# Attention, then two gated layers: scores of two of four sequences from fp16 pairs, thresholds of three sequences moved to VectorE

## The chip, the core and the metric

One NeuronCore of a Trainium2 chip runs the whole program. TensorE (PE) multiplies matrices into PSUM; VectorE (DVE), ScalarE (ACT) and GpSimd (POOL) do the elementwise work; SyncE (SP) issues the DMAs. Each engine takes its own instructions in the order in which they stand, and waits on semaphores for the others. The metric is the device time of one execution in microseconds; lower is better.

## The reference, cut to what matters

```python
scores = q @ k.T / sqrt(64)                  # 4 sequences, 8 heads, 576 positions, 64 wide
keep   = scores >= rowmax(scores) - tau      # tau = 0.02
attn   = where(keep, exp(scores - rowmax), 0); attn /= sum(attn)
x      = (attn @ v) laid out as 2304 tokens x 512
h = x @ w_in;  g = h * clip(h + 3, 0, 6) / 6;  x = g @ w_out      # 512 -> 2048 -> 512
h = x @ w_in2; g = max(h, 0) ** 2;             out = g @ w_out2
```

A score that falls on the wrong side of the threshold changes an output row, so the scores need close to fp32 accuracy. One pass of 16-bit products isn't enough for that: wherever 16-bit numbers are multiplied, each operand is split into a high and a low part.

## The kernel before, in words

**Attention.** A unit is one pair of heads of one sequence, 16 units in all, four to a sequence (`u.b` is the sequence, counted from 0). A unit has nine jobs: four tiles of 128 query rows for each head, and one job for the last 64 rows of both heads. A job is `scores` (PE, tile `s`), `soft1` (DVE takes the row minimum `nm` of the negated scores, the threshold `thr` is `nm` plus tau, ACT takes the exponential `e`), `soft2` (DVE masks and sums; ACT and POOL split the result into two fp16 parts `p`, a DMA transposes them into `pt`), and five jobs later `av` (PE, tile `o`).

For sequence one the scores are plain fp32 products (L291). For sequences two to four `prep_steps` (L187) transposes k and q on PE (`tps`) and splits each from PSUM into a high part (ACT) and a low part (DVE) of type fp32r; high times high, low times high and high times low are then two matmuls for each half of the columns, so four in a job and eight in the job of the last rows (L295): 40 in a unit. Two DMAs copy the high part of k onto the other 64 partitions. `prep_v` (L238) finds the largest |v| of the unit with a reduce, an fp32 matmul (`vm`) and a second reduce, and makes a power of two of it, `vsc`.

**The layers.** They run block by block (layer 1 and layer 2 of sequence one, then of sequence two, ...), each in groups: `hidden` (PE, tile `hp`, 24 matmuls of 288 columns, fp16 pairs) and `output` (PE, tile `y`, 24 matmuls). At the end of layer 1, the boundary below, VectorE has to take the largest |y| of each of the four tiles of `ya` (L730) and of all (L733), PE spreads it over the partitions (L119), DVE makes a power of two of it (L121, L126, L737), and only then ACT and DVE split `ya` into `x` (L386, L387), without which the first `hp` of layer 2 can't begin.

**The order.** The loops issue some attention jobs between the steps of the layers (`attn_to`). A scheduler that works from a simulated timeline then orders each engine's instructions, so an instruction without waiting inputs can stand far ahead of its place in the source. Up to 378 us the weights are decoded as well (L544 to L623): 32 blocks through ACT, DVE and POOL. Scores, `hp` and `y` share three PSUM buffers, `tps`, `vm`, `o` and the rest two others.

Of the kernel before, what the change touches and what calls it, by code (L numbers as in the profile page):

```python
# [39 lines left out]
def attention_moe_moe_kernel(  # L40
# [195 lines left out]
    vscs = {}  # L236

    def prep_v(u):  # L238

# [11 lines left out]
        nc.vector.tensor_scalar(out=sc, in0=sc, scalar1=2.0 ** -100, scalar2=2.0 ** -13, op0=ALU.max, op1=ALU.mult)
        nc.vector.reciprocal(out=sc, in_=sc)
        nc.vector.tensor_scalar(out=sc.bitcast(I32), in0=sc.bitcast(I32), scalar1=0x7f800000, scalar2=None, op0=ALU.bitwise_and)
# [603 lines left out]
```

## Time and profile before

| | us |
|---|---|
| median of 3 runs | 1099.24 (1097.81 to 1100.69) |
| the profiled execution | 1097.44 |
| its span, first to last instruction | 1095.7 |
| PE busy | 1014.6 (93%) |
| ACT, DVE, POOL busy | 654.4, 642.9, 502.0 |

The page divides the span into 40 slices; a digit is the busy share in tenths. "Granted clock" is the share of full speed that TensorE was given. A line of a timeline says when an instruction started, how long it took and, in brackets, how long its engine had been idle and what ended that. Times of consecutive matmuls overlap in the records, so what a matmul costs is read from one start to the next.

### The profile page before, as it was taken

The numbers are of one execution on the slowest core, as the hardware profiler recorded it, in microseconds if no ns is written. First come the engines' busy times: TensorE is split into PE (matmuls) and PEld (weight loads), VectorE is DVE, ScalarE is ACT, GpSimd is POOL, SyncE is SP. The second block draws the span as 40 slices with busy tenths as digits, with TensorE's granted clock in tenths as the row PEclk, the third lists the DMA queues.
The fourth block names the chain that finished last, engine by engine and source line by source line (L and its number), as shares of the span: only waits on it lengthen the run. The fifth ranks groups of instructions, "written<-read, shape, count | busy, mean of one in ns | idle before, by whom it ended". The sixth has DMA issues, their size and how long they took to land.

```text
span 1095.7 us, 23283 instructions
## 1 busy us (share of the span) xinstructions
PE 1014.6 (93%) x9248; PEld 819.2 (75%) x9248; DVE 642.9 (59%) x1344; ACT 654.4 (60%) x1128; POOL 502.0 (46%) x629
## 2 busy tenths in 40 slices
PE   6877698897987999999999999999999999998998
PEld 4655476676776888888788888888788887776776
DVE  6885789889778875455855554555834231233122
ACT  5896798877887875655675555655654243313222
POOL 5886656755656754344355334443444222212111
PEclk9999799898988999999999999999999999999999
DMA  9999689896877686656565555555464342222211
GB/s 271 186 181 234 197 313 289 253 215 175 198 190 213 144 200 168 146 119 150 127 139 125 141 143 140 132 130 133 94 139 116 105 121 83 92 77 78 78 39 44
DMA packets 258748, 167.58 MB, mean 153 GB/s; under 512 B 215888, under 2 KB 228176, under 8 KB 258640
## 3 DMA queue, kind: packets, MB, share of 16 engines
q1 hardware_dynamic: 257072, 165.71, 60.3%
q8 instruction: 72, 1.18, 0.4%
q10 hardware_dynamic: 1568, 0.39, 0.2%
q14 instruction: 36, 0.29, 0.1%
HBM read 98.57 MB, written 21.50 MB: 110 GB/s over the span
## 4 chain that ended last, share of the span: by engine, by line
PE 72%; DVE 13%; DMA 7%; ACT 5%; issue 2%; POOL 1%; ACTq 0%; POOLq 0%; DVEq 0%
PE hp L685 30%; PE y L722 30%; PE s L295 4%; PE o L350 4%; DMA pt<-p 2%; DVE nm L301 2%; DVE wc L620 2%; DMA wd<-in_moe_w_out_dram 1%; DVE e L318 1%; DMA vraw<-in_v_dram 1%; PE s L291 1%; DVE ya L728 1%; PE tps L180 1%; DMA pt<-wpo 1%; DMA wd<-in_moe_w_in_dram 1%
## 5 line engine op out<-in xcount | busy, mean ns | idle before, releaser
L685 PE MATMUL hp<-x,wpi 128*128 128x288 f16 x3072 | 405.7, 291 | 13.8 <-ACT wpi L622 5.2
L685 PEld LDWEIGHTS <-wpi 128*128 128x128 f16 x3072 | 300.1, 99 | 94.7 <-ACT wpi L622 5.5
L722 PEld LDWEIGHTS <-wpo 128*128 128x128 f16 x3072 | 297.5, 99 | 92.7 <-DVE e L318 7.9
L722 PE MATMUL y<-gh,wpo 128*128 128x288 f16 x2048 | 338.7, 288 | 15.9 <-DVE e L318 7.5
L696 POOL TENSOR_TENSOR gl<-g,gh 128x576 f16<-128x576 f32 x128 | 168.6, 1318 | 299.6 <-ACT gh L695 298.9
L722 PE MATMUL y<-gl,wpo 128*128 128x288 f16 x1024 | 209.2, 288 | 0.0
L301 DVE TENSOR_REDUCE nm<-s 128x1 f32<-128x576 f32 x144 | 107.6, 750 | 58.7 <-PE s L295 55.3
L728 DVE SCALAR_TENSOR_TENSOR ya<-y,yq,ya 128x576 f32<-128x576 f32 (+1 forms) x97 | 77.9, 809 | 97.5 <-PE y L722 97.3
L326 POOL TENSOR_TENSOR p<-e,p 128x512 f16<-128x512 f32 x108 | 127.2, 1178 | 0.0
L695 ACT ACTIVATE gh<-g 128x576 f16<-128x576 f32 x128 | 86.9, 680 | 56.0 <-DVE g L693 27.9
L318 DVE SCALAR_TENSOR_TENSOR e<-s,thr,e 128x576 f32<-128x576 f32 x108 | 87.9, 814 | 38.9 <-ACT e L311 38.0
L324 ACT ACTIVATE p<-e 128x576 f16<-128x576 f32 x108 | 73.5, 681 | 51.3 <-DVE e L318 41.1
L350 PE MATMUL o<-v,pt 128*128 128x64 f16 (+1 forms) x2016 | 90.5, 200 | 12.2 <-ACT os L357 4.0
L350 PEld LDWEIGHTS <-pt 128*128 128x128 f16 x2016 | 80.6, 101 | 24.1 <-issue 9.3
L295 PE MATMUL s<-k_st,q_st 128*128 128x288 f32 x480 | 94.5, 320 | 0.6 <-DVE g L690 0.3
L693 DVE TENSOR_TENSOR g<-g,hp 128x576 f32<-128x576 f32 x64 | 48.0, 750 | 64.6 <-ACT g L692 64.4
L690 DVE SCALAR_TENSOR_TENSOR g<-g,r_w,hp 128x576 f32<-128x576 f32 x64 | 51.9, 810 | 57.8 <-ACT g L689 57.7
L689 ACT ACTIVATE g<-hp,r_h,aq 128x576 f32<-128x576 f32 x64 | 52.9, 829 | 53.7 <-PE hp L685 52.9
L692 ACT ACTIVATE g<-hp,r_w 128x576 f32<-128x576 f32 x64 | 47.1, 736 | 57.1 <-PE hp L685 55.9
L311 ACT ACTIVATE e<-s,nm 128x576 f32<-128x576 f32 x108 | 78.5, 727 | 0.4
L325 POOL TENSOR_TENSOR p<-e,p 128x64 f16<-128x64 f32 x108 | 35.2, 326 | 95.0 <-issue 59.2
L333 POOL TENSOR_SCALAR sm<-sm,vsc 128x2 f32<-128x2 f32 (+1 forms) x80 | 23.0, 287 | 112.7 <-DVE e L318 99.7
(127 smaller groups left out, 1138.5 us busy)
## 6 DMA issues: line engine op xcount, KB each, us to landing
wpi<-scr SPq DMA_DIRECT2D x48, 512.0 KB, 3.7
wpo<-scr SPq DMA_DIRECT2D x48, 512.0 KB, 4.1
wd<-in_moe_w_in_dram SPq DMA_DIRECT2D x16, 1024.0 KB, 7.2
wd<-in_moe_w_out_dram SPq DMA_DIRECT2D x16, 1024.0 KB, 6.9
scr<-wpi SPq DMA_DIRECT2D x16, 512.0 KB, 6.9
scr<-wpo SPq DMA_DIRECT2D x16, 512.0 KB, 5.0
kraw<-in_k_dram SPq DMA_DIRECT2D x16, 256.0 KB, 4.3
vraw<-in_v_dram SPq DMA_DIRECT2D x16, 256.0 KB, 3.2
```

Source lines behind the costliest of these rows:

```text
L295: nc.tensor.matmul(s[:, half, 0:HALF], lhsT=u.qs[sl][:, cs], rhs=u.ks[sl][:, kk, c], start=i == 0, stop=i == len(ops) - 1)
L301: nc.vector.tensor_reduce(out=j.nm, in_=j.s, axis=AX.XY, op=ALU.min)
L311: nc.scalar.activation(out=j.e, in_=j.s, func=AF.Exp, bias=j.nm, scale=-1.0)
L318: nc.vector.scalar_tensor_tensor(out=j.e, in0=j.s, scalar=j.thr, in1=j.e, op0=ALU.is_le, op1=ALU.mult, accum_out=u.sm[:, col:col + 1])
L324: nc.scalar.activation(out=p16[:, 0:S], in_=e, func=AF.Copy)
L326: nc.gpsimd.tensor_tensor(out=p16[:, S + TAIL:], in0=e[:, 0:NT * P], in1=p16[:, 0:NT * P], op=ALU.subtract)
L350: nc.tensor.matmul(o[:, n * w:n * w + w], lhsT=j.pt[:, c, :], rhs=vv[:, hs, vc, :], start=i == 0, stop=i == len(ops) - 1)
L685: last_hp[0] = nc.tensor.matmul(hp[:, a, 0:HALF], lhsT=wsl(tag, "i", f, w, c), rhs=x[c][:, a * HALF:(a + 1) * HALF], start=i == 0, stop=i ...
L695: nc.scalar.activation(out=gh, in_=gf, func=AF.Copy)
L696: nc.gpsimd.tensor_tensor(out=gl, in0=gf, in1=gh, op=ALU.subtract)
L722: nc.tensor.matmul(a[:, k_, 0:HALF], lhsT=wsl(tag, "o", f, w, e), rhs=g[f][:, k_ * HALF:(k_ + 1) * HALF], start=i == 0, stop=i == len(ops) ...
L728: nc.vector.scalar_tensor_tensor(out=y, in0=av_, scalar=yq, in1=y, op0=ALU.mult, op1=ALU.add)
```

## The change

Sequences three and four (`u.b > 1`) take a new path, `prep_16`. It finds the largest |k|, |q| and |v| of the unit (three reduces, one of the tails, two small maxima, three fp32 matmuls where one was, one reduce over all three), makes three powers of two, and splits k and q, still from PSUM, into fp16 parts that are scaled by them. The minimum of the scores then has to be scaled back: `nt` is one VectorE instruction with two results, the bias of the exponential and the threshold. For sequence two the threshold is a VectorE addition. ScalarE's threshold instruction (L305) is gone from all three. The k copies are issued after the q parts, two steps later than before. Matmul counts of the scores stay the same.

```diff
+        if u.b > 1:
+            yield from prep_16(u)
+            return
...
+    def amax(out, x):
+        nc.vector.tensor_reduce(out=out, in_=x, ..., op=ALU.max, apply_absolute_value=True)
+    def prep_16(u):
+        am = st.tile([P, 4], F32, name="am4", bufs=2)
+        amax(am[:, 0:1], u.k.rearrange("p t h d -> p (t h d)"))
+        amax(am[:, 1:2], u.q.rearrange("p t h d -> p (t h d)"))
+        yield
+        tails_v(u)
+        amax(am[:, 3:4], tl[u.b][:, 2 * u.p:2 * u.p + 2].rearrange("p h d -> p (h d)"))
+        amax(am[:, 2:3], u.v.rearrange("p h t d -> p (h t d)"))
+        for i in range(2):
+            nc.vector.tensor_tensor(out=am[own[i], i:i + 1], in0=am[own[i], i:i + 1], in1=am[own[i], 3:4], op=ALU.max)
+        yield
+        a = ps_a.tile([P, 512], F32, tag="acc", name="vm")
+        for i in range(3):
+            nc.tensor.matmul(a[:, i * P:i * P + P], lhsT=am[:, i:i + 1].to_broadcast([P, P]), rhs=ident, start=True, stop=True)
+        sc = st.tile([P, 3], F32, name="sc3", bufs=2)
+        nc.vector.tensor_reduce(out=sc, in_=a[:, 0:3 * P].rearrange("p (n c) -> p n c", n=3), axis=AX.X, op=ALU.max)
+        scale_of(sc)
...
+        for part in (0, 1):
+            a = transpose_part(u, "k", part)
+            c0, n = cols(part)
+            for h in range(2):
+                kh = u.ks[h][own[h], 0, c0:c0 + n]
+                nc.scalar.activation(out=kh, in_=a[own[h], 0:n], func=AF.Copy, scale=sc[own[h], 0:1])
+                nc.vector.scalar_tensor_tensor(out=u.ks[h][own[h], 1, c0:c0 + n], in0=a[own[h], 0:n], scalar=sc[own[h], 0:1], in1=kh, op0=ALU.mult, op1=ALU.subtract)
+            yield
...
+        for h in range(2):
+            nc.sync.dma_start(out=u.ks[h][own[1 - h], 0, :], in_=u.ks[h][own[h], 0, :])
+        split_v(u)
...
     def soft1(j):
...
-        else:
-            nc.scalar.activation(out=j.thr, in_=j.nm, func=AF.Identity, bias=tau_a)
...
+        if u.b > 1:
+            if j.n == 0:
+                nc.vector.reciprocal(out=u.fac[:, 0:1], in_=u.both)
+                nc.vector.tensor_scalar(out=u.add[:, 1:2], in0=u.both, scalar1=tau_a, scalar2=None, op0=ALU.mult)
+                nc.vector.tensor_scalar(out=u.neg, in0=u.fac[:, 0:1], scalar1=-1.0, scalar2=None, op0=ALU.mult)
+            nt = st.tile([P, 2], F32, name="nt")
+            nc.vector.scalar_tensor_tensor(out=nt, in0=u.fac, scalar=j.nm, in1=u.add, op0=ALU.mult, op1=ALU.add)
+            j.thr = nt[:, 1:2]
+            nc.scalar.activation(out=j.e, in_=j.s, func=AF.Exp, bias=nt[:, 0:1], scale=u.neg)
+            return
...
+            nc.vector.tensor_scalar(out=j.thr, in0=j.nm, scalar1=tau_a, scalar2=None, op0=ALU.add)
         nc.scalar.activation(out=j.e, in_=j.s, func=AF.Exp, bias=j.nm, scale=-1.0)
```

Up to about 125 us the order on every engine is the same. From there the scheduler orders all of them anew. The prediction speaks of the end of layer 1 of sequences two and three. On VectorE, before, these rows stand at the end of layer 1 of sequence two, between the last reduce of `ya` and `ex`, the power of two that the layer waits for (`gm<-y` is the largest of all, `mx<-vm` the same after PE has spread it):

```order
L249 TENSOR_REDUCE vsc<-vm 128x1
L301 TENSOR_REDUCE nm<-s 128x1 x2
L733 TENSOR_REDUCE gm<-y_7556 128x1
L251 TENSOR_SCALAR vsc<-vsc 128x1
L318 SCALAR_TENSOR_TENSOR e,sm<-s,thr,e 128x576
L712 MEMSET y_13828 128x1
L252 RECIPROCAL vsc<-vsc 128x1
L318 SCALAR_TENSOR_TENSOR e,sm<-s,thr,e 128x576
L121 TENSOR_REDUCE mx<-vm 128x1
L253 TENSOR_SCALAR vsc<-vsc 128x1
L361 TENSOR_TENSOR os<-o,sm 128x2x64
L126 TENSOR_SCALAR ex<-mx 128x1
```

After the change the same stretch of VectorE begins with these rows (`am<-vraw` and `am<-kraw` are new reduces, L302 makes a low part of k, L397 is `nt`, L828 is the old L733):

```order
L825 TENSOR_REDUCE y_7636<-ya 128x1
L385 TENSOR_REDUCE nm<-s 128x1
L302 SCALAR_TENSOR_TENSOR k_5685<-tps,sc_7586,k_5685 64x320
L397 SCALAR_TENSOR_TENSOR nt<-fac_96,nm,add_98 128x2
L251 TENSOR_REDUCE am_9060<-vraw 128x1
L385 TENSOR_REDUCE nm<-s 128x1
L828 TENSOR_REDUCE gm<-y_7636 128x1
```

and goes on with these, to `ex` (L413 is the mask, the old L318; L312 makes a low part of q):

```order
L397 SCALAR_TENSOR_TENSOR nt<-fac_96,nm,add_98 128x2
L302 SCALAR_TENSOR_TENSOR k_5686<-tps,sc_7586,k_5686 64x320
L413 SCALAR_TENSOR_TENSOR e,sm<-s,nt,e 128x576
L251 TENSOR_REDUCE am_9060<-kraw 128x1
L397 SCALAR_TENSOR_TENSOR nt<-fac_96,nm,add_98 128x2
L807 MEMSET y_13996 128x1
L122 TENSOR_REDUCE mx<-vm 128x1
L413 SCALAR_TENSOR_TENSOR e,sm<-s,nt,e 128x576
L312 SCALAR_TENSOR_TENSOR q_5683<-tps,sq,q_5683 64x256
L127 TENSOR_SCALAR ex<-mx 128x1
```

Two low parts of k, two reduces over 512 and 640 columns and three `nt` have come in between; the second mask and a low part of q now stand between `mx` and `ex`; the steps of `vsc` have gone to another place. At the end of layer 1 of sequence three, VectorE has this, without the two reduces:

```order
L302 SCALAR_TENSOR_TENSOR k_5685<-tps,sc_11229,k_5685 64x320
L397 SCALAR_TENSOR_TENSOR nt<-fac_96,nm,add_98 128x2
L385 TENSOR_REDUCE nm<-s 128x1
L828 TENSOR_REDUCE gm<-y_11277 128x1
L397 SCALAR_TENSOR_TENSOR nt<-fac_96,nm,add_98 128x2
L302 SCALAR_TENSOR_TENSOR k_5686<-tps,sc_11229,k_5686 64x320
L397 SCALAR_TENSOR_TENSOR nt<-fac_96,nm,add_98 128x2
L413 SCALAR_TENSOR_TENSOR e,sm<-s,nt,e 128x576
L122 TENSOR_REDUCE mx<-vm 128x1
L413 SCALAR_TENSOR_TENSOR e,sm<-s,nt,e 128x576
L312 SCALAR_TENSOR_TENSOR q_5683<-tps,sq,q_5683 64x256
L127 TENSOR_SCALAR ex<-mx 128x1
```

Before, that place had the same rows as at the end of layer 1 of sequence two. On PE, 70 matmuls of `o` stood between `vm` (L119) and the first `hp` of layer 2 at both places; after, two transposes (`tps`) and 28 of `o` stand there, and the other 42 come behind the first `hp`.

## Rows read from the trace of the kernel before

**Rows 1.** The page: busy us (share of the span) and instructions of each engine.
```profile
PE 1014.6 (93%) x9248; PEld 819.2 (75%) x9248; DVE 642.9 (59%) x1344; ACT 654.4 (60%) x1128; POOL 502.0 (46%) x629
```

**Rows 2.** Stretches: length; busy us (instructions) of each engine; clock; DMA share, GB/s.
```profile
125.00:400.00 275.00, 242.08 (x2176) 194.61 (x2177) 225.63 (x482) 221.08 (x352) 170.99 (x176) 0.92 0.85 226
400.00:860.00 460.00, 454.74 (x4369) 376.46 (x4367) 258.64 (x547) 268.85 (x491) 200.68 (x250) 0.99 0.56 134
```

**Rows 3.** PE's waits from 400 to 860 us: us in total, times, longest.
```profile
PE vm L119 <- DVE vsc L251: 3.9, 2, 1.9
```

**Rows 4.** PE's waits from 125 to 400 us.
```profile
PE vm L119 <- DVE gm L546: 8.3, 2, 5.8
PE y L722 <- DVE e L318: 7.5, 4, 5.2
PE y L722 <- ACT wpo L622: 4.5, 1, 4.5
```

**Rows 5.** PE's timeline from 221 us: start us, us, instruction.
```profile
221.64 0.38 PE L119 MATMUL vm<-ident_m,gm 128*128 128x128 f32 x2
221.86 3.10 PE L685 MATMUL hp<-x,wpi 128*128 128x288 f16 x24
224.71 0.79 PE L295 MATMUL s<-k_st,q_st 128*128 128x288 f32 x4
225.34 1.07 PE L584 MATMUL gr<-wpi 128*128 128x128 f16 x16
```

**Rows 6.** Groups by shape: count, busy us, mean ns, idle before, what ended it.
```profile
L685 PEld LDWEIGHTS <-wpi 128*128 128x128 f16 x3072 | 300.1, 99 | 94.7 <-ACT wpi L622 5.5 <-issue 5.2 <-DVE e L318 4.0
L295 PEld LDWEIGHTS s<-k_st,q_st 128*128 128x128 f32 x480 | 70.0, 191 | 4.0 <-PE hp L685 0.6 <-DVE g L693 0.5 <-DVE e L318 0.3
L305 ACT ACTIVATE thr<-nm,tau_a 128x1 f32<-128x1 f32 x108 | 31.6, 293 | 64.5 <-DVE nm L301 64.0
L243 DVE TENSOR_REDUCE am<-vraw 128x1 f32<-128x640 f32 x16 | 13.1, 816 | 11.8 <-DMA vraw<-in_v_dram 11.7
L220 DVE TENSOR_TENSOR k_st<-tps,k_st 64x320 fp32r<-64x320 f32 x24 | 11.6, 485 | 1.3 <-ACT k_st L219 0.9
L676 DVE TENSOR_SCALAR aq<-e_w,r_w 128x1 f32<-128x1 f32 x16 | 3.0, 200 | 0.1
```

**Rows 7.** DMA issues: count, KB each, median us to landing.
```profile
k_st<-k_st SPq DMA_DIRECT2D x24, 144.0 KB, 4.2
```

**Rows 8.** DVE's timeline, end of layer 1 of sequence two.
```profile
536.15 0.28 DVE L249 TENSOR_REDUCE vsc<-vm 128x1 f32<-128x128 f32 x1
536.35 1.41 DVE L301 TENSOR_REDUCE nm<-s 128x1 f32<-128x576 f32 x2
537.68 0.15 DVE L733 TENSOR_REDUCE gm<-y 128x1 f32<-128x5 f32 x1
...
537.80 0.81 DVE L318 SCALAR_TENSOR_TENSOR e<-s,thr,e 128x576 f32<-128x576 f32 x1
...
539.34 0.28 DVE L121 TENSOR_REDUCE mx<-vm 128x1 f32<-128x128 f32 x1
...
539.98 0.16 DVE L737 RECIPROCAL sx<-ex 128x1 f32<-128x1 f32 x1
```

**Rows 9.** PE's timeline, same place.
```profile
539.68 2.95 PE L350 MATMUL o<-v,pt 128*128 128x64 f16 x42 [0.24 <-DVE vsc L253]
542.47 0.65 PE L685 MATMUL hp<-x,wpi 128*128 128x288 f16 x4
```

**Rows 10.** ACT's timeline, same place.
```profile
541.50 2.76 ACT L386 ACTIVATE x<-ya,sx 128x576 f16<-128x576 f32 x4
```

**Rows 11.** All engines over that place (columns as in rows 2).
```profile
533.00:545.00 12.00, 9.82 (x118) 9.01 (x116) 11.73 (x39) 8.59 (x16) 4.81 (x8) 0.86 0.65 154
```

**Rows 12.** DVE's timeline: a small instruction with two SBUF inputs.
```profile
542.15 0.62 DVE L677 TENSOR_TENSOR aq<-aq,ex 128x1 f32<-128x1 f32 x1
```

**Rows 13.** POOL's timeline at the same time.
```profile
541.60 1.16 POOL L326 TENSOR_TENSOR p<-e,p 128x512 f16<-128x512 f32 x1
```

More of the change, by code (lines that the diff above doesn't have):

```diff
@@ L148, in setup @@
                 nc.gpsimd.memset(k_st[h][i][own[1 - h], 1, :].bitcast(F32), 0.0)
+        for i in range(2):
+            nc.gpsimd.memset(fac[i], 1.0)
+            nc.gpsimd.memset(add[i], 0.0)
     class Unit:
@@ new lines, in prep_16 @@
+    def prep_16(u):
[6 more added lines that the diff above has]
+        amax(am[:, 2:3], u.v.rearrange("p h t d -> p (h t d)"))
+        for i in range(2):
+            nc.vector.tensor_tensor(out=am[own[i], i:i + 1], in0=am[own[i], i:i + 1], in1=am[own[i], 3:4], op=ALU.max)
[6 more added lines that the diff above has]
+        scale_of(sc)
+        if u.p == 0:
+            vscs[u.b] = st.tile([P, NPAIR], F32, name="vsc", bufs=2)
+        u.vsc = vscs[u.b][:, u.p:u.p + 1]
+        nc.vector.tensor_copy(out=u.vsc, in_=sc[:, 2:3])
+        u.fac, u.add = fac[u.i % 2], add[u.i % 2]
+        u.neg = st.tile([P, 1], F32, name="neg", bufs=2)
+        sq = st.tile([P, 1], F32, name="sq", bufs=2)
+        both = st.tile([P, 1], F32, name="both", bufs=2)
+        nc.vector.tensor_scalar(out=sq, in0=sc[:, 1:2], scalar1=qs, scalar2=None, op0=ALU.mult)
+        nc.vector.tensor_scalar(out=both, in0=sc[:, 0:1], scalar1=sc[:, 1:2], scalar2=2.0 ** 126, op0=ALU.mult, op1=ALU.min)
+        nc.vector.tensor_scalar(out=both, in0=both, scalar1=2.0 ** -126, scalar2=None, op0=ALU.max)
+        u.both = both
+        i = u.i % 2
+        if i not in q16:
+            q16[i] = [big.tile([P, QZ], F16, tag=f"q{h}{i}", name=f"q16{h}{i}") for h in range(2)]
+            k16[i] = [big.tile([P, 2, S], F16, tag=f"k{h}{i}", name=f"k16{h}{i}") for h in range(2)]
+            for h in range(2):
+                nc.gpsimd.memset(q16[i][h][:, NT * P:NT * P + 64], 0.0)
+                nc.gpsimd.memset(q16[i][h][:, QZ - 64:], 0.0)
+                nc.gpsimd.memset(k16[i][h][own[1 - h], 1, :], 0.0)
+        u.qs, u.ks = q16[i], k16[i]
+        yield
[6 more added lines that the diff above has]
+                nc.vector.scalar_tensor_tensor(out=u.ks[h][own[h], 1, c0:c0 + n], in0=a[own[h], 0:n], scalar=sc[own[h], 0:1], in1=kh, op0=ALU.mult, op1=ALU.subtract)
+            yield
+        for part in (0, 1):
+            a = transpose_part(u, "q", part)
+            c0, n = cols(part)
+            for h in range(2):
+                for a0, d0, m in ((0, c0, 2 * P), (2 * P, NT * P + 64, n - 2 * P)):
+                    if m > 0:
+                        qh = u.qs[h][own[h], d0:d0 + m]
+                        nc.scalar.activation(out=qh, in_=a[own[h], a0:a0 + m], func=AF.Copy, scale=sq[own[h]])
+                        nc.vector.scalar_tensor_tensor(out=u.qs[h][own[1 - h], d0:d0 + m], in0=a[own[h], a0:a0 + m], scalar=sq[own[h]], in1=qh, op0=ALU.mult, op1=ALU.subtract)
+            yield
+        for h in range(2):
+            nc.sync.dma_start(out=u.ks[h][own[1 - h], 0, :], in_=u.ks[h][own[h], 0, :])
+        split_v(u)
@@ L250, in prep_v, with split_v @@
         yield
[L251 to L253 removed]
+        scale_of(sc)
+        split_v(u)
+    def split_v(u):
+        sc = u.vsc
+        vin = u.v.rearrange("p h t d -> p (h t d)")
         v16 = at.tile([P, 2, 2, NT + 1, D], F16, name="v16")
```

32 lines of the change are left out of this document (20 added, 12 removed).

## The prediction

> **What bounds the kernel.** I read the page first, then the busy time by stretches, then who ended PE's waits in each, then the timelines where it waits longest. PE is busy 93% of the span [rows 1]. From 400 to 860 us, where most of the changed work runs, it is busy 454.7 of 460 us, VectorE 258.6, ScalarE 268.9 [rows 2], and of PE's 5.3 us of waiting 3.9 are two waits for one chain of small VectorE steps, at the two ends of layer 1 [rows 3]. There only a shorter list of matmuls, or a shorter end of layer 1, makes the kernel faster. From 125 to 400 us, where the weights are decoded, the reader is to see another picture: PE 242 of 275 us at a granted clock of 0.92, VectorE 226, ScalarE 221 [rows 2]. PE waits there for VectorE (8.3 and 7.5 us) more than for ScalarE (4.5) [rows 4]. Before 125 us the two programs are the same, and after 860 us no attention runs.
>
> **Matmuls of the scores.** 8 units of 40 matmuls, 320, go from fp32r to fp16. What one costs now is read from starts, since its record, like that of its weight load, overlaps its neighbours. In rows 5 the 24 hp and the four scores behind them take 225.34 - 221.86 = 3.48 us; of that the hp took 2.85 up to the scores' start, which lies 0.03 us into the last hp, so 23 steps in 2.82 us, 0.1226 us each. The four scores then cost (3.48 - 24 x 0.1226) / 4 = 0.134 us. An fp16 matmul of as many columns is 0.1226. So the gain is 0.0115 us each, 3.7 us together. Bounds: nothing (if scores of fp16 keep 0.134), and the difference of the weight loads, 191 against 99 ns [rows 6], 320 x 0.092 = 29 us, if the loads set the pace. The start times say they don't, and I take 3.7.
>
> The Trainium skill says the opposite of this in effect: TensorE: Matmul & The Clock Gate, Weight-path perf modes, has it that the fast weight load is on for 128 weights of any type but FP32. The trace agrees on the loads themselves (191 against 99 ns), and by the rule alone the sum would be 29 us smaller; it is a rival below.
>
> **The three maxima on PE.** Two more fp32 matmuls of 128 columns a unit. One, two records, takes 221.86 - 221.64 = 0.22 us [rows 5]: 8 x 2 x 0.22 = 3.5 us more. Bounds 0 (where they fall into a wait of PE) and 3.5; in a stretch with 99% PE they are paid. PE's own balance is -0.2.
>
> **ScalarE's threshold and what replaces it.** 108 instructions of 0.293 us leave ScalarE [rows 6], 31.6 us. For 72 jobs the exponential, which waited for nm and stood behind the threshold on ScalarE, now waits for nt on VectorE; behind it on ScalarE stand the ReLUs and casts of hp, for which PE's y waits. nt is like L676 (0.20 us, 0.12 where the next one overlaps it) [rows 6], so the path from nm to e is a tenth shorter or longer. From 400 to 860 us this hides under PE, as the old path did: PE waited for no mask there [rows 3].
>
> nt has two inputs in SBUF (fac and add), and L677 is the row of such an instruction: 0.62 us for 128x1, and it ended at 542.77, just when POOL's L326 ended (541.60 + 1.16 = 542.76) [rows 12, 13]. So nt costs 0.12 to 0.8. With POOL busy 201 of 460 us [rows 2] and half of 1.16 left on average, 0.44 x 0.58 = 0.25 us more; 72 x 0.25 = 18 us of VectorE, hidden where it has 200 us to spare, but not at the ends of layer 1; I take 0.2 there. SBUF — State Buffer, SBUF: two separate sides (the Trainium skill), states it as a rule that speaks against this change: a VectorE instruction with two SBUF inputs and a GpSimd one that reads SBUF exclude each other for their whole length. These rows agree.
>
> **More VectorE work in each unit.** Reduces of k and q (512 of 640 columns of the 0.816 us of L243 [rows 6], about 0.6 each), of the tails, a wider reduce of vm, a dozen small ones: about 2.8 us a unit, 22 us in all. VectorE goes from 259 to about 295 of 460 us: hidden, price nothing; uncovered it would be the same 22 us. These reduces wait for loads: L243's 16 lost 11.7 us so [rows 6]. Everything behind such a wait on VectorE waits too, masks and PSUM releases among it. 16 more of them may add another 11.7 us of VectorE idling; off the ends of layer 1 I price it at nothing, with 5 as the upper bound.
>
> **End of layer 1, sequence two.** VectorE is busy 11.73 of 12 us there, PE 9.8 at clock 0.86 [rows 11]. Before, from the last reduce of ya to sx took 539.98 - 536.15 = 3.83 us [rows 8]. The order shows what comes in; prices are durations less the 0.08 us by which neighbours overlap (two nm start 1.33 us before gm, and last 1.41): two low parts of k, 2 x 0.41 [rows 6]; three nt, 3 x 0.12; reduces of v and k, 0.74 + 0.57; a low part of q, about 0.4: 2.9 us. Out go the vsc reduce, 0.2 [rows 8], and four small ones that the rest of the 3.83 us leaves 0.4 for. Net +2.3. ScalarE gives some back: x started at 541.50 [rows 10], 1.4 us after sx was there, behind older work that is done by the later time; I take 1.1 back: +1.2. Of the 70 o that filled PE's wait, 42 (from 539.68 to 542.47, up to the first hp [rows 9]) come later; at 64 of 288 columns of 0.123 us they are 1.1 us of work, less 0.2 for two transposes that fill in: +0.9. POOL's hold on three nt: +0.6 (0 to 2). The two reduces wait for loads just then: by L243 0.73 each, taken at half, +0.7 (0 to 4). Together +3.4, bounds 0 and +8.
>
> **End of layer 1, sequence three.** The same without the reduces: 0.82 + 0.36 + 0.4 - 0.6 = +1.0, less 1.0 from ScalarE, +0.9 for o, +0.6 for nt: +1.5, bounds -1 and +4. For sequence one, where PE lost most of the 8.3 us [rows 4], two threshold additions and a reduce of q come into the chain and other rows leave it: +0.5, bounds -3 and +4.
>
> **From 125 to 400 us.** VectorE, at 82%, gets 36 additions (0.12 to 0.20, 4 to 7 us) and the first two preparations (5.6 us); ScalarE, at 80%, loses 36 x 0.293 = 10.6 us. If all of ScalarE's relief reached PE: -10; all of VectorE's load: +12. PE waits more for VectorE there [rows 4], so I take +1.
>
> **Hidden.** Ten zero fills on POOL, once, and the tails' copies as before: POOL is 44% busy. The k copies, two DMAs a unit, half as large, are issued two jobs later; one lands in 4.2 us [rows 7], a job comes every 6.4 us (460 us for 72), and two jobs lie between. Without that cover: 8 x 4.2 us.
>
> **Sum.** -0.2 + 3.4 + 1.5 + 0.5 + 1.0 = +6.2 us on the profiled execution's 1097.44: 1103.6. The median of the runs, 1099.24, is 1.8 above it; I add about half of that, since one run says little of where the median lies: 1104.5, given as 1105.
>
> **Rivals.**
> - *ScalarE's relief decides (faster).* From 125 to 400 us the 10.6 us leave the engine on which decoding, casts and exponentials queue, masks come earlier, and PE's 7.5 us of waiting for masks and 4.5 for wpo shrink. For it: ScalarE is at 80%, and e waits for ScalarE. Against: what PE waits for longest is VectorE. It decides where more than about 10 us of waits go: 1097.4 + 5.2 - 10 to -12 = about 1092. Chance 0.17.
> - *Weight loads set the pace (much faster).* -29 + 3.5 + 5 = 1077. Against it: 0.134 us between scores, with loads of 0.191 recorded. Chance 0.03.
> - *The ends of layer 1 don't lengthen (no change).* The reduces find their loads landed, POOL stands idle at nt, ScalarE's slack takes the whole 2.3 us. What is left is -0.2 on PE and up to 2 of o: 1096 to 1102, say 1099. For it: those waits have slack of 1.4 us on ScalarE. Chance 0.25.
> - *VectorE starves PE (slower still).* Waits for loads and POOL's hold on nt push masks and releases back in the 90%-busy stretches: 5 + 18 x 0.3 more, 1110 to 1118. Chance 0.12.
> - Forecast, 1101 to 1110: chance 0.43.
>
> About 0.3%, 3.3 us, is what a measurement of this kernel can tell from no change: faster is below 1096, slower above 1102.5. Faster: 0.03 + 0.17 = 0.20. Same: 0.25 and a small part of the forecast, 0.28. Slower: 0.52. The range 1094 to 1113 leaves out the second rival, about a third of the first and half of the last.
>
> **What would show it.** Right: four scores in a row at 0.123 us; three vm matmuls a unit at 0.66; PE's wait for L120 at the ends of layer 1 grown from 1.9 us to 3 or more, with nt and am rows inside it; nt of 0.2 to 0.8 us, long ones ending with a POOL instruction; PE busy still 99% from 400 to 860 us. Wrong: scores at less than 0.12 us, an end of layer 1 no longer than before, or a stretch from 125 to 400 us that moved by more than 5 us either way.

## The result, and the profile after

The changed kernel takes 1113.55 us (median of 6, 1109.96 to 1117.86) against 1099.97 us (6 runs). By the medians it is 13.6 us slower; the ratio of the two sets of runs is 1.0134, 95% interval 1.0107 to 1.016. I had forecast 1105 with a range of 1094 to 1113, so the direction was right, the size too small by more than half, and the time lies just above the range. The profiled execution took 1113.96 us, its span is 1112.2, which is 16.5 more than the span before.

The page, against [rows 1], and two windows, against [rows 2]:

```profile
PE 1023.0 (92%) x9280; PEld 817.5 (74%) x9280; DVE 706.0 (63%) x1546; ACT 641.1 (58%) x1020; POOL 509.7 (46%) x645
```

```profile
400.00:860.00 460.00, 447.34 (x4279) 362.35 (x4277) 304.32 (x684) 258.51 (x421) 196.37 (x246) 0.98 0.55 128
125.00:400.00 275.00, 240.09 (x2155) 192.33 (x2156) 237.29 (x538) 210.66 (x301) 175.73 (x185) 0.93 0.81 225
```

VectorE has 63 us more, ScalarE 13 less, and PE lost 7 us of work from 400 to 860. PE's waits there, against [rows 3]:

```profile
PE vm L120 <- DVE nt L397: 6.3, 2, 3.5
PE tps L183 <- DVE os L456: 1.9, 2, 1.2
PE o L445 <- DVE mx L122: 1.6, 2, 1.0
```

**Where the time went.** VectorE adds 97 times into `ya` (L728 before, L823 after), in the same order in every run. The start of such a sum in one trace less its start in the trace before says how late the program is at that place. The marks used are the sums that start at 336.08, 410.48, 534.03, 593.13, 776.05, 833.40, 988.31 and 1035.74 us before, and at 337.00, 414.97, 539.58, 603.73, 787.36, 848.96, 1003.86 and 1052.42 after. The third, fifth and seventh are the last sums of layer 1 of sequences two, three and four; what follows each is called "end two", "end three" and "end four" here. Up to 336 us the loss is 0.92 us. Each column is the lateness added between two marks, in the one profiled execution of each kernel:

| us | 336-410 | 410-534 | end two (534-593) | 593-776 | end three (776-833) | 833-988 | end four (988-1036) |
|---|---|---|---|---|---|---|---|
| after | +3.6 | +1.1 | +5.05 | +0.7 | +4.25 | 0.0 | +1.1 |
| e1 max with one input | +1.8 | +1.3 | +5.0 | +0.8 | +3.2 | 0.0 | -1.7 |
| e2 idle matmuls ahead | +5.2 | +1.1 | +5.25 | +1.1 | +3.5 | 0.0 | 0.0 |
| f1 idle matmuls, longer | +1.9 | +1.2 | +6.45 | +0.6 | +3.45 | 0.0 | -0.2 |
| e3 before, thresholds only | -2.0 | +0.9 | +1.7 | +0.15 | +1.6 | +0.1 | 0.0 |
| e4 no maxima of q and k | +2.4 | +0.4 | +3.45 | +0.7 | +3.0 | 0.0 | +0.9 |
| f2 nt with one input | +3.3 | -0.2 | +6.6 | -0.3 | +3.8 | 0.0 | +0.8 |
| f3 thresholds two on ScalarE | +4.0 | +1.0 | +5.1 | -0.5 | +4.2 | 0.0 | -0.3 |
| f4 bf16 maxima | +2.6 | +0.5 | +3.6 | -0.7 | +3.75 | 0.0 | +1.1 |
| g2 two reduces behind x | +1.9 | +1.2 | +5.1 | +0.7 | +3.3 | 0.0 | -1.7 |
| g5 two reduces ahead of x | +2.1 | +1.3 | +8.3 | +0.7 | +6.1 | 0.0 | +0.9 |
| h1 constant scale of x | -0.2 | +2.6 | +5.0 | +1.9 | +2.7 | 0.0 | +0.8 |
| g4 before, two behind x | +0.2 | +0.3 | 0.0 | 0.0 | +0.2 | -0.05 | 0.0 |
| g6 before, two ahead of x | +0.15 | 0.0 | +3.7 | 0.0 | +3.7 | -0.1 | -1.7 |
| h2 before, constant scale of x | +0.3 | +0.9 | -1.35 | +0.8 | -1.0 | +0.05 | +0.8 |

Most of the loss, 12.9 of 16.7 us, sits at three places: between 336 and 410 us, at end two and at end three. The other runs are explained below.

**End two.** VectorE's timeline, where [rows 8] has the same place before:

```profile
539.58 0.81 DVE L823 SCALAR_TENSOR_TENSOR ya<-y,yq,ya 128x576 f32<-128x576 f32 x1
...
541.03 0.74 DVE L825 TENSOR_REDUCE y<-ya 128x1 f32<-128x576 f32 x1
...
542.36 0.54 DVE L302 SCALAR_TENSOR_TENSOR k<-tps,sc,k 64x320 f16<-64x320 f32 x1
542.81 0.20 DVE L397 SCALAR_TENSOR_TENSOR nt<-fac,nm,add 128x2 f32<-128x2 f32 x1
542.94 0.81 DVE L251 TENSOR_REDUCE am<-vraw 128x1 f32<-128x640 f32 x1
...
545.97 0.68 DVE L251 TENSOR_REDUCE am<-kraw 128x1 f32<-128x512 f32 x1
...
547.75 0.48 DVE L312 SCALAR_TENSOR_TENSOR q<-tps,sq,q 64x256 f16<-64x256 f32 x1
...
548.45 0.16 DVE L832 RECIPROCAL sx<-ex 128x1 f32<-128x1 f32 x1
...
552.22 1.53 DVE L482 SCALAR_TENSOR_TENSOR x<-ya,sx,x 128x576 f16<-128x576 f32 x2
```

From the end of the last sum (539.58 + 0.81) to the end of x's last low part (552.22 + 1.53) it is 13.36 us. Before, the same two rows give 10.96:

```profile
534.03 0.82 DVE L728 SCALAR_TENSOR_TENSOR ya<-y,yq,ya 128x576 f32<-128x576 f32 x1 [0.17 <-PE y L722]
...
543.55 2.26 DVE L387 SCALAR_TENSOR_TENSOR x<-ya,sx,x 128x576 f16<-128x576 f32 x3
```

That is +2.40 us of VectorE ahead of x. At end three the same span goes from 10.84 to 12.69, +1.85, by these rows before and after:

```profile
776.05 0.82 DVE L728 SCALAR_TENSOR_TENSOR ya<-y,yq,ya 128x576 f32<-128x576 f32 x1 [0.17 <-PE y L722]
...
784.72 3.00 DVE L387 SCALAR_TENSOR_TENSOR x<-ya,sx,x 128x576 f16<-128x576 f32 x4
```

```profile
787.36 0.81 DVE L823 SCALAR_TENSOR_TENSOR ya<-y,yq,ya 128x576 f32<-128x576 f32 x1
...
799.33 1.53 DVE L482 SCALAR_TENSOR_TENSOR x<-ya,sx,x 128x576 f16<-128x576 f32 x2
```

What these ends cost PE is read from its busy time between the marks of the table (columns as in rows 2). End two and end three, before, then after:

```profile
534.03:593.13 59.10, 56.41 (x542) 47.08 (x540) 37.12 (x94) 41.70 (x78) 30.81 (x40) 0.97 0.62 144
776.05:833.40 57.35, 54.78 (x533) 45.80 (x532) 31.00 (x75) 36.95 (x66) 29.96 (x38) 0.97 0.53 125
```

```profile
539.58:603.73 64.15, 57.77 (x543) 46.04 (x543) 46.50 (x124) 41.65 (x70) 27.65 (x37) 0.92 0.57 134
787.36:848.96 61.60, 56.89 (x529) 45.07 (x529) 36.59 (x91) 37.87 (x62) 27.61 (x37) 0.92 0.48 112
```

At end two PE stands idle for 64.15 - 57.77 = 6.4 us, before for 2.7; at end three for 4.7, before for 2.6. So 3.7 of the 5.05 us and 2.1 of the 4.25 are PE waiting longer, and 1.4 and 2.1 are its matmuls taking longer, at a mean granted clock of 0.92 where it was 0.97. PE's timeline at end two, against [rows 9]:

```profile
544.62 0.77 PE L120 MATMUL vm<-ident_s,gm 128*128 128x128 f32 x2 [3.53 <-DVE nt L397]
...
547.04 1.65 PE L445 MATMUL o<-v,pt 128*128 128x64 f16 x28 [1.04 <-DVE mx L122]
...
550.33 1.14 PE L780 MATMUL hp<-x,wpi 128*128 128x288 f16 x4
```

Only 28 of the 70 `o` fill the wait now, and four hp take 1.14 us where they took 0.65 [rows 9]. The granted clock was at its lower level, 1.2 GHz of 2.4; PE had stood idle for 3.53 and 1.04 us just before. All engines in the ten microseconds from the first hp on, before and after:

```profile
542.50:552.50 10.00, 9.49 (x79) 7.70 (x77) 9.40 (x19) 9.38 (x20) 6.06 (x9) 1.00 0.65 141
```

```profile
550.30:560.30 10.00, 9.09 (x87) 6.97 (x87) 9.77 (x27) 5.57 (x11) 1.63 (x4) 0.88 0.66 134
```

### The profile page after: what moved, and what is told of

Read it like the earlier page. It is cut to its first block, busy times and chain, and to the rows that moved or that the text cites. A ratio compares the mean times of both kernels' runs of the same rounds, so it can differ in the third digit from the quotient of the medians.

```text
span 1112.2 us, 23479 instructions
## 1 busy us (share of the span) xinstructions
PE 1023.0 (92%) x9280; PEld 817.5 (74%) x9280; DVE 706.0 (63%) x1546; ACT 641.1 (58%) x1020; POOL 509.7 (46%) x645
## 4 chain that ended last, share of the span: by engine, by line
PE 62%; DVE 19%; ACT 7%; DMA 6%; issue 3%; POOL 3%; SPq 0%; ACTq 0%; POOLq 0%; DVEq 0%
PE hp L780 27%; PE y L817 26%; PE o L445 3%; PE s L379 3%; DVE nm L385 2%; DVE e L413 2%; DVE wc L715 2%; DMA wd<-in_moe_w_in_dram 2%; DVE ya L823 1%; DMA wd<-in_moe_w_out_dram 1%; DVE g L639 1%; DMA vraw<-in_v_dram 1%; PE s L375 1%; DVE am L251 1%; DMA pt<-wpo 1%
## 5 line engine op out<-in xcount | busy, mean ns | idle before, releaser
L823 DVE SCALAR_TENSOR_TENSOR ya<-y,yq,ya 128x576 f32<-128x576 f32 (+1 forms) x97 | 77.5, 807 | 83.8 <-PE y L817 83.4
L445 PEld LDWEIGHTS <-pt 128*128 128x128 f16 x2016 | 86.2, 101 | 25.7 <-issue 13.7
L413 DVE SCALAR_TENSOR_TENSOR e<-s,nt,e 128x576 f32<-128x576 f32 x72 | 58.8, 817 | 57.7 <-ACT e L399 57.6
L399 ACT ACTIVATE e<-s,nt,neg 128x576 f32<-128x576 f32 x72 | 59.5, 828 | 45.6 <-DVE nt L397 44.4
L428 POOL TENSOR_SCALAR sm<-sm,vsc 128x2 f32<-128x2 f32 (+1 forms) x80 | 25.8, 322 | 86.2 <-DVE e L413 75.2
L375 PE MATMUL s<-xr,ya 128*128 128x288 f32 x144 | 49.6, 479 | 6.8 <-DVE g L413 6.6
```

What stands on the lines that cost most here:

```text
L375: nc.tensor.matmul(s[:, half, 0:HALF], lhsT=u.qf[:, t, :], rhs=u.kf[:, c], start=True, stop=True)
L399: nc.scalar.activation(out=j.e, in_=j.s, func=AF.Exp, bias=nt[:, 0:1], scale=u.neg)
L413: nc.vector.scalar_tensor_tensor(out=j.e, in0=j.s, scalar=j.thr, in1=j.e, op0=ALU.is_le, op1=ALU.mult, accum_out=u.sm[:, col:col + 1])
L445: nc.tensor.matmul(o[:, n * w:n * w + w], lhsT=j.pt[:, c, :], rhs=vv[:, hs, vc, :], start=i == 0, stop=i == len(ops) - 1)
L823: nc.vector.scalar_tensor_tensor(out=y, in0=av_, scalar=yq, in1=y, op0=ALU.mult, op1=ALU.add)
```

## The experiments

Edits are shown shortened. A bracket behind a time has the 95% interval of its ratio to the kernel before, or, where it is in microseconds, the fastest and the slowest run.

### A small maximum held by POOL (e1)

In the trace after, a maximum of 64x1 with two inputs in SBUF took 2.92 us; behind it stood the mask for which PE waited 3.1 us. VectorE, POOL at the same time, and PE's waits from 340 to 420 us:

```profile
380.20 2.92 DVE L266 TENSOR_TENSOR am<-am 64x1 f32<-64x1 f32 x1
383.15 0.82 DVE L413 SCALAR_TENSOR_TENSOR e<-s,thr,e 128x576 f32<-128x576 f32 x1
```

```profile
378.36 2.13 POOL L718 TENSOR_TENSOR wpo<-wc,wpo 128x1024 f16<-128x1024 f32 x1
380.44 1.28 POOL L791 TENSOR_TENSOR gl<-g,gh 128x576 f16<-128x576 f32 x1
381.67 0.32 POOL L420 TENSOR_TENSOR p<-e,p 128x64 f16<-128x64 f32 x1
381.94 1.16 POOL L421 TENSOR_TENSOR p<-e,p 128x512 f16<-128x512 f32 x1
```

```profile
PE y L817 <- DVE e L413: 4.1, 2, 3.1
```

The hold ends when POOL's fourth instruction in a row ends (381.94 + 1.16 = 383.10). The trace of e2 (below), with the same instructions up to there, has it again: 2.90 us, ending 0.03 us behind the same POOL instruction.

```
-nc.vector.tensor_tensor(out=am[own[i], i:i+1], in0=am[own[i], i:i+1], in1=am[own[i], 3:4], op=max)
+nc.vector.tensor_reduce(out=am[own[i], i:i+1], in_=am[own[i], i:4:3-i], op=max)
```

> The changed kernel with one instruction replaced: the maximum of a unit's k (or q) column and its tails column is a reduce over the two columns (one input in SBUF) and no longer an operation with two inputs. Theory A (the loss sits at a few places: the two ends of layer 1, and one hold of a small VectorE instruction with two SBUF inputs by POOL at 380 us): the instruction of 2.92 us at 380.2 us falls to under 0.3, PE's wait of 3.1 us for the mask behind it goes, and the time falls by 2 to 4 us, to about 1110.5. Theory B (63 us more of VectorE's time slow the kernel evenly): 5 us less of 706 on VectorE, under 1 us of the total.

Measured: 1108.59 us (1105.54 to 1111.17), ratio 1.0072 (1.0049 to 1.0095). The instruction and the wait, in its own trace:

```profile
377.46 0.15 DVE L266 TENSOR_REDUCE am<-am 64x1 f32<-64x2 f32 x1
```

```profile
PE y L817 <- DVE e L413: 1.4, 2, 1.0
```

The stretch to 410 us loses 1.8 instead of 3.6. Nothing else in the program moved: every other instruction stands where it stood. So 1.7 us are the hold's in this pair. Four more runs with e1's maximum and the same order up to there (f1, g1, g2, g5) lose 1.9 to 2.1 us in this stretch; e2, with the hold, loses 5.2. The medians differ by 5.0 us, the two profiled executions by 8.4. Of these 8.4 the table gives 3.1 to the time up to 336 us, 1.0 to end three and 2.8 to end four, where the instructions are the same; at the ends that is the clock (below).

### What is idle on PE, and its clock (e2, f1, and end four)

```
+[nc.tensor.matmul(a[:, P:P+HALF], lhsT=xh[0][:, 0:P], rhs=xh[0][:, 0:HALF]) for _ in range(24)]   # f1: 26, on e1
 nc.tensor.matmul(a[:, 0:P], lhsT=am.to_broadcast([P, P]), rhs=ident_s)                               # vm
+[the same 14 times]                                                                                  # f1 only
```

> The changed kernel with 24 idle matmuls of 288 columns (their result is not read) on PE ahead of the maximum at the ends of layer 1 of sequences two and three, where PE waited 3.5 and 2.8 us and its granted clock was 0.50 for some 10 us from then on. Theory A (of the 5.5 and 4.4 us lost at these ends, 2 to 3 each are work done at half the clock): the clock stays at 1.00 for most of it and 1.5 to 2.5 us come back at each end, 3 to 5 together, about 1109.5. Theory B (the chain of VectorE steps alone sets the ends, or the loss is spread evenly): no change, or up to 2 us slower for the added matmuls.

Measured: 1115.15 us, ratio 1.0135 (1.0112 to 1.0157); end two +5.25, end three +3.5. No gain: the clock fell later and was at 0.50 when the first hp came.

> The changed kernel with the one-input maximum (as in the run e1, 1108.6 us) and with idle matmuls of 288 columns on PE at the ends of layer 1 of sequences two and three, 26 ahead of the maximum and 14 behind it (their results are not read). In the run e2, with 24 ahead alone, the clock fell only later, and was at 0.50 again when the first hp came. Theory A (1 to 2 us of each end are hp matmuls at half the clock): PE's clock is 1.00 when the first hp starts, and from there to the steady stretch nothing is lost; the end of sequence two costs 3.5 to 4 us more than before the change instead of 5.0, that of sequence three 2 to 2.5 instead of 3.0; 1106. Theory B (VectorE's chain alone sets the ends): both ends as long as in e1, 1108 to 1110.

Measured: 1111.54 us, 1.0105 (1.0077 to 1.0134); end two +6.45, end three +3.45. The clock was full, and the end no shorter. Ten microseconds from the first hp on, and PE's waits in them:

```profile
545.60:555.60 10.00, 7.99 (x77) 6.28 (x73) 9.71 (x29) 6.23 (x12) 1.99 (x4) 1.00 0.83 171
```

```profile
554.41 0.66 PE L379 MATMUL s<-k,q 128*128 128x288 f16 x4 [1.49 <-DVE e L413]
555.91 2.32 PE L780 MATMUL hp<-x,wpi 128*128 128x288 f16 x9 [0.83 <-DVE g L788]
```

PE at full clock now waits for VectorE (busy 9.71 of 10 us), so theory A's gain did not come. The test isn't clean, though: the added matmuls also changed the order, and from the last sum to x's last low part it is 15.35 us here, in e1 13.37. What the clock costs at end two is not shown by it.

Where VectorE is not the bound, the clock has its full price. End four has no attention beside it, and the waits in it are the same in before, after and e1 (1.9 us for gm, 1.6 for x). The six microseconds from the first hp on, in these three:

```profile
992.20:998.20 6.00, 5.98 (x36) 4.15 (x36) 3.00 (x4) 1.97 (x3) 0.00 (x0) 0.72 0.01 3
```

```profile
1007.80:1013.80 6.00, 6.00 (x27) 3.84 (x27) 2.96 (x4) 1.92 (x3) 0.00 (x0) 0.52 0.00 1
```

```profile
1002.20:1008.20 6.00, 6.00 (x50) 4.79 (x50) 2.94 (x4) 2.54 (x4) 0.00 (x0) 1.00 0.00 0
```

6 x (0.72 - 0.52) = 1.2 us more in the run after, 6 x (1.00 - 0.72) = 1.7 us less in e1: the table has +1.1 and -1.7. PE and VectorE have the same instructions in the same order there in all the runs of the table, and end four lies anywhere between these two values. So the +1.1 belongs to that execution and not to the change. After and e1 also differ so at end three, by 1.04 us with the same instructions. The ten microseconds from the first hp on:

```profile
797.40:807.40 10.00, 10.00 (x91) 7.58 (x91) 8.57 (x22) 6.90 (x13) 3.18 (x6) 0.77 0.43 82
```

```profile
792.70:802.70 10.00, 10.00 (x102) 8.03 (x102) 8.73 (x22) 7.02 (x13) 3.17 (x6) 0.87 0.47 86
```

10 x (0.87 - 0.77) = 1.0. Before, this window is at 1.00.

### Ahead of x or behind it (g2, g4, g5, g6, h1, h2, g1, g3)

```
g2 (on e1), g4 (on before), behind split_scaled(...):
+[nc.vector.tensor_reduce(out=dm, in_=xl[NC-1], op=max) for _ in range(2 if b in (1, 2) else 0)]
g5 (on e1), g6 (on before), ahead of the reduce gm:
+[nc.vector.tensor_reduce(out=y4[:, e:e+1], in_=ya[:, e, :], op=max, abs) for _ in range(2 if b in (1, 2) else 0)]
```

> The changed kernel with the one-input maximum, and two reduces of 576 columns more on VectorE (their results are not read) at the ends of layer 1 of sequences two and three, placed behind x, so outside the chain from the last reduce of ya to sx. Theory C (VectorE's whole work is the bound there): 2 x 0.7 us at each end, +2 to +3 in all, about 1111. Theory D (only the chain up to sx counts): no change, 1108.6.

> The kernel before with two reduces of 576 columns more on VectorE (their results are not read) behind x at the ends of layer 1 of sequences two and three. Theory C (VectorE is the bound at these ends before the change as well): +1 to +1.4 us at each, 1102.5 to 1103.5. If VectorE has that much room there before the change, no change: 1100.4, and the slope begins only with the changed kernel's added work.

> The changed kernel with the one-input maximum (run e1), and the last reduce of ya done three times over (two more of 0.66 us each) at the ends of layer 1 of sequences two and three, so inside the chain from ya to sx, where the run g2 had two reduces behind x. Theory D (what counts on VectorE is what stands ahead of the last low part of x, and PE falls to half its clock while it waits): +1.3 us at each end at least, up to 2 with the clock, +2.5 to +4 in all, about 1112; in g2 the same length of reduces cost 0.1 us. Theory E (the ends cost what they cost because the order there is another, whatever stands in the chain): under 0.5 us at each end.

> The kernel before with the same two reduces in the chain of the ends of sequences two and three. Theory D: +1.3 to +2 us at each end, +2.5 to +4 in all, about 1103.5; g4 had two behind x, at no cost. Theory E: under 0.5 us at each end.

Measured: g2 1111.99 us (1.0086 to 1.0143) and g4 1099.58 us (0.9996 to 1.003): their ends cost what e1's and before's cost, within 0.2 us. (g2's median, 3.4 us above e1's, would fit theory C, but its six runs lie between 1105.77 and 1116.57 and the profiled one, the fastest, shows nothing of it at the ends.) The two reduces in g2 stand where they should, and VectorE was busy there:

```profile
547.77 1.53 DVE L482 SCALAR_TENSOR_TENSOR x<-ya,sx,x 128x576 f16<-128x576 f32 x2
...
552.09 1.40 DVE L833 TENSOR_REDUCE dm<-x 128x1 f32<-128x576 f16 x2
```

g5: 1116.61 us (1.0132 to 1.0188), g6: 1108.63 us (1.0057 to 1.0114). 1.32 us put ahead of x cost 3.3 and 2.9 us in g5 (8.3 - 5.0, 6.1 - 3.2), 3.7 at both ends in g6; behind x they cost nothing. Theory C, that VectorE's whole work there counts, falls; theory D stands in so far as what is ahead of x counts. But 1.32 us is not all that came ahead of x: the order changed with it, and at end two it is 16.78 us from the last sum to x's last low part in g5 and 14.29 in g6, +3.4 and +3.3 (at end three +4.4 and +3.4). At end two that is about what was lost.

```
h1 (on e1), h2 (on before), for sequences two and three; the maximum over all of ya and the steps to sx are left out:
+nc.gpsimd.memset(xsc["e"], 16.0); nc.gpsimd.memset(s2, 0.0625)      # instead of gm, vm, mx, ex, sx
```

> The changed kernel with the one-input maximum (run e1), and at the ends of layer 1 of sequences two and three the scale of x is a constant (the maximum of ya over partitions, its matmul and the steps to sx are left out), so that nothing stands between the last ya and x but VectorE's queue. Theory D: in e1 these ends cost 5.0 and 3.2 us more than before the change; without the chain what was added to it cannot count, and against the kernel before with the same constant (run h2) both ends cost under 1.5 us more each. Theory E, or VectorE's load: the differences of 5.0 and 3.2 stay. The time falls by 6 to 10 us against e1.

> The kernel before with the same constant scale of x at the ends of layer 1 of sequences two and three (the maximum and the steps to sx left out). It is the partner of h1: the difference of the two kernels at these ends is what is asked for. By its own rows PE waits 1.9 us at each end and loses about 1 to 1.5 us to the half clock: 2 to 4 us less at each, about 1094.

Measured: h1 1113.47 us (1.011 to 1.0161), h2 1098.66 us (0.9983 to 1.0021). Neither fell as expected: h1 is 4.9 us above e1, and h2 gained 1.35 and 1.0 at its ends, not 2 to 4. h1's ends still cost 5.0 and 2.7, so the two kernels differ by 6.4 and 3.7 without the chain as well. Theory D in the form that only the chain from ya to sx counts falls. PE in h1:

```profile
548.79 4.72 PE L780 MATMUL hp<-x,wpi 128*128 128x288 f16 x21 [6.11 <-DVE e L413]
```

x had its scale at once, and PE waited 6.1 us for a mask: that is for VectorE's queue of minima, low parts and reduces between the last sum and what PE needs next (x, or a mask that frees a tile). How much of that is the added work and how much the new order of it (theory E), these two runs don't separate.

Two attempts took work off that queue: two of x's four low parts made by ScalarE and POOL (in g3 at the end of sequence one as well).

```
+if c in (2, 3): nc.scalar.activation(out=src[c], in_=src[c], scale=s); nc.gpsimd.tensor_tensor(out=xl[c], in0=src[c], in1=xh[c], op=subtract)
```

> The changed kernel with the one-input maximum (run e1), and at the ends of layer 1 of sequences two and three two of the four low parts of x made by ScalarE (scaling in place) and POOL in place of VectorE. In the run f1 PE's clock was full at these ends and they cost as much as ever, with VectorE busy 23.45 of 24 us. Theory C (VectorE's whole work there is the bound, each us of it costs about one us): 2 x 0.75 us less, 1 to 1.5 us back at each end, about 1106. Theory D (only the chain up to sx counts; x comes behind it): no change, or 1 us later at each end for POOL's slower subtraction: 1108 to 1111.

> The kernel before with two of the four low parts of x made by ScalarE and POOL in place of VectorE at the ends of layer 1 of sequences one to three. VectorE is busy 11.73 of 12 us there in the kernel before too. Theory C: 1 to 1.5 us back at each of three ends, 1096 to 1097, faster than both kernels. Theory D: no change, or up to 1 us later at each end, 1100 to 1103.

Measured: g1 1111.09 us (1.0082 to 1.0129), ends +4.55 and +4.7 (e1: +5.0 and +3.2), by the median not clearly different from e1; g3 1107.74 us (1.0044 to 1.0092), +1.6 and +4.2, slower. No gain; x was complete later: by its last low part 2.4 and 2.0 us later than in e1, 4.0 and 5.1 later than before.

### The parts one by one (e3, f3, f2, e4, f4)

```
e3 (on before)   -nc.scalar.activation(out=j.thr, in_=j.nm, func=Identity, bias=tau_a)
                 +nc.vector.tensor_scalar(out=j.thr, in0=j.nm, scalar1=tau_a, op0=add)
f3 (on e1)       the same in reverse, for sequence two
f2 (on e1)       nt by two tensor_scalar of nm, with fac and add as scalars
e4 (on after)    -amax(k), amax(q), amax(tails), the maxima with tails   +memset(am[:, 0:2], 8.0)
f4 (on e1)       lhsT=am.bitcast(BF16)[:, 2*i+1:2*i+2].to_broadcast([P, P]), rhs=ident_b
```

> The kernel before with one line changed: the thresholds of sequences two to four are added by VectorE, not ScalarE; scores stay fp32r. Theory A: three additions of 0.12 to 0.2 us come into each end of layer 1, the rest is hidden: 0 to +3 us, about 1101.5, and the two steps of 4 to 5 us that the changed kernel shows at the ends are not there. Theory B: 108 x 0.2 = 22 us more on VectorE, a third of the 63, so a third of the loss, +5. The rival of relief on ScalarE: 31.6 us leave ScalarE, 1092.

Measured: 1101.72 us, 1.0017 (1.0002 to 1.0032). Theory A's total is right, and ScalarE's relief isn't worth 8 us. But each end cost 1.6, not 0.5: the last of x's low parts stood behind POOL (at end two it took 1.95 us; POOL's L264 ran from 544.20 to 545.81), and three took 3.41 us, 2.26 before. From the last sum to x's last low part it is 1.8 us more than before at both ends, about what was lost.

> The changed kernel with the one-input maximum, and the thresholds of sequence two added by ScalarE again. Theory A (these 36 additions cost nothing to speak of on either engine, up to one in the end of sequence one): within 2 us of 1108.6. Rival (ScalarE's relief, or VectorE's load, decides between 125 and 400 us): 10.6 us more on ScalarE and 7.4 less on VectorE move the stretch by more than 3 us, one way or the other.

Measured: 1118.13 us (1.0135 to 1.0189), 9.5 above e1: theory A fails, and the stretch moved by more than the rival's 3 us. The sum at 336.08 us comes 9.1 us late, in e1 2.2 early. PE waited 8.9 us for gm L641 there, in e1 1.2, in the kernel before 8.3 [rows 4]. The order is another too, and 4.6 of the 9.1 us are there at the first sum already, at 170 us; whether the moved additions or the order do it stays open.

> The changed kernel with the one-input maximum, and nt made by two operations that each read one tensor (nm) with a scalar per partition, in place of one with two tensors (fac and add) from SBUF. Theory A (POOL's hold on nt is hidden where PE is busy 99%): nt takes 0.15 to 0.25 us each, VectorE's time for them falls from 28.6 us to 20 to 25, and the kernel's time stays within 1.5 us of 1108.6. Theory B (the hold on nt delays masks and so PE all along): no nt above 0.3 us and 4 to 6 us less, 1103.

Measured: 1112.68 us (1.0075 to 1.0135). The two operations never take more than 0.22 us, and together 29.5 us, as much as one with its holds (28.6): no saving, and the ends grow. A miss in the estimate; the hold on nt isn't priced by it.

> The changed kernel without the maxima of q, k and their tails (the scale of q and k comes from a constant 8 instead, so this part of the computation is left out; the three matmuls, the scales and all else stay). Theory A: the hold at 380 us goes (3 us) and the end of layer 1 of sequence two loses a reduce of 0.6 us, while the end of sequence three, which has no such reduce in it, keeps its 4 us: 1107 to 1110. Theory B: 19 of 63 us leave VectorE, so 4 to 5 us come back, spread evenly over 380 to 860 us: 1109, with no step at 380 us.

Measured: 1109.65 us (1.0046 to 1.0107). End two is 1.6 us shorter than after, of which I had expected 0.6; end three is 1.25 shorter, where nothing was expected (e1 has 1.0 of that by the clock alone). The time fits theory A and theory B alike.

> The changed kernel with the one-input maximum, and the three maxima of a unit on PE from the upper halves of their fp32 numbers, as bf16 (the maximum is cut to 8 bits, the scales are powers of two as before). My prediction's term of +3.5 us for two more fp32 matmuls a unit says: a vm falls from two records in 0.22 us to one in about 0.06, 24 of them give back 24 x 0.16 = 3.8 us where PE is busy 99%: 1104.8. Rival (PE waits somewhere behind them anyway): within 1.5 us of 1108.6.

Measured: 1107.8 us (1.005 to 1.0102), no different from e1 by the median. From 593 to 776 us, where PE is full, it gives back 1.5 us (+0.8 to -0.7); of the group, after and f4:

```profile
L270 PE MATMUL vm<-ident,am 128*128 128x128 f32 x48 | 6.7, 275 | 0.0
```

```profile
L270 PE MATMUL vm<-ident_b,am 128*128 128x128 bf16 x24 | 2.6, 219 | 0.0
```

Nine maxima of three units lie in that stretch: 9 x 0.16 = 1.5. The term of the three maxima is right where PE is the bound.

## Why the prediction was wrong, by its steps

**Matmuls of the scores: right.** Four scores in a row:

```profile
386.98 0.65 PE L379 MATMUL s<-k,q 128*128 128x288 f16 x4
387.47 1.27 PE L445 MATMUL o<-v,pt 128*128 128x128 f16 x25
```

(387.47 - 386.98) / 4 = 0.1225 us; I had 0.1226. By the fast weight load of the Trainium skill (TensorE: Matmul & The Clock Gate, Weight-path perf modes) I had a rival of 29 us less; the loads did become faster (99 ns where they took 191 [rows 6]), and the scores didn't follow.

**Threshold and nt: right in total, partly by luck.** 72 nt take 28.6 us, 397 ns on average, from 0.20 to 1.31; I had 0.12 to 0.8 and 18 us of holds on top of 0.15 each, 29. The base was too low and the holds, at 0.20 a base, are 14 us: two errors that cancel. 19 of the 72 take over 0.4 us, and each of these ends 0.02 us behind a POOL instruction. At the ends they took 0.20, so the +0.6 there was not.

**Loads: not there.** The reduces' waits for loads fell from 11.7 us [rows 6] to 2.6 + 1.3 + 3.1 = 7.0, and none stood in the ends; so +0.7 was not.

```profile
L251 DVE TENSOR_REDUCE am<-vraw 128x1 f32<-128x640 f32 x16 | 13.0, 815 | 3.8 <-DMA vraw<-in_v_dram 2.6 <-POOL gl L791 1.0 <-POOL sm L428 0.2
...
L251 DVE TENSOR_REDUCE am<-qraw 128x1 f32<-128x512 f32 x8 | 5.5, 682 | 3.1 <-DMA qraw<-in_q_dram 3.1
L251 DVE TENSOR_REDUCE am<-kraw 128x1 f32<-128x512 f32 x8 | 5.5, 682 | 1.4 <-DMA kraw<-in_k_dram 1.3
```

**End of layer 1, sequence two: +3.4, measured +5.05.** The net addition to VectorE up to sx, +2.3, was 2.9. Then I took 1.1 back for ScalarE. It was there: x's high parts start at 548.96, 0.35 us behind sx. But hp needs the low parts too, and VectorE makes them; only 0.5 came back (sx is 2.9 us later from the last reduce on, x's end 2.4). The terms for nt and loads, 1.3 together, were not there, so the sum came nearer than its parts.

**End of layer 1, sequence three: +1.5, measured +4.25. This is the step that failed most.** I counted 1.0 of VectorE and gave all of it back to ScalarE; at x's last low part 1.85 were left (two low parts of q stand ahead of it, not one). And PE's clock was no term at any end, although [rows 11] showed 0.86: half of the 4.25 is PE's matmuls taking longer, at a clock of 0.92 where it was 0.97, and e1, with the same instructions, lost 1.0 less.

**End of layer 1, sequence one: +0.5, measured +0.8, by luck.** That is between the sums at 252.06 and 336.08 us. I started from PE's wait of 8.3 us for gm L546 [rows 4]. From 125 to 400 us that wait (gm L641 after) shrank to 1.8, and the one for gm L682, 3.7 before as gm L587, grew to 8.3.

**From 125 to 400 us: +1.** 0.9 at 336 us, then 3.6 more. Of these 1.7 were the maximum of k and of its tail, one of "a dozen small ones" that I priced as hidden. I had bounded the hold on nt by half of one POOL instruction; the maximum has two SBUF inputs like nt, and was held over POOL's whole run. The Trainium skill (SBUF — State Buffer, SBUF: two separate sides) has the two exclude each other for a whole instruction; here the trace shows three further POOL instructions passing before VectorE got its turn. For the rest, f3 moved this stretch by over 9 us with the thresholds of one sequence and the order that came with them, so that +1 had no ground in how the stretch works.

**Hidden elsewhere: right.** 833 to 988 us loses nothing, 593 to 776 us 0.7 with 45 us more on VectorE from 400 to 860. The sign that I had named, PE busy 99% there, did not hold: it is 447.34 of 460 us, 97%, for the most part by the longer waits at the two ends.

**The rival "VectorE starves PE".** The time lies in its range, 1110 to 1118, to which I gave 0.12. Its two causes are not what is seen: the waits for loads became shorter, and the holds on nt have no shown price. The hold that cost time was another, and it was priced at nothing.

**Sum.** By the table, with its 0.92 up to 336 us: 0.9 + 3.6 + 1.1 + 5.05 + 0.7 + 4.25 + 1.1 = 16.7 of the span's 16.5; I had 6.2. Of the 10.5 us between, ends two and three are 1.7 and 2.75 beyond their terms, the hold is 1.7, and end four's 1.1 is one execution's clock. The 1.1 and 0.7 at 410 to 534 and 593 to 776 us, where I had -0.2 for PE, have no shown cause, nor has the rest before 410 us. That VectorE's work ahead of x lengthens the ends is shown by g5 and g6 against g2 and g4; that it is all that lengthened them after the change is not, since no run brought the ends back to their old length.

## What to carry to other kernels

Find the places where the bound engine runs dry, and count what the helper engine has queued ahead of what ends the dry spell: there 1.3 us, with what the new order put ahead beside it, cost 3, and the same work right behind it nothing. Follow that queue to the last instruction that the bound engine needs, here x's low parts, and not only to the scale they wait for. Give the matrix engine's clock behind each such spell a term of its own, with a width of 1 to 3 us. When one instruction is priced by a hold, look for all others with the same operands.
